# Recurrence and top-capacity experts on one core: 17 thresholds in the last search step, the recount dropped, five result buffers instead of three

## The chip, the core and the metric

The kernel runs on one core of a Trainium2 chip. Its engines run in parallel, each through its own queue in order: TensorE (PE for matmuls, PEld for weight loads), VectorE (DVE), ScalarE (ACT), GpSimd (POOL, which here issues the indirect transfers) and SyncE (SP). They wait for one another by semaphores. The metric is the device time of the whole kernel in microseconds, the median of several runs.

## The reference

A gated recurrence over 4 sequences of 5056 rows of 256, then a mixture of 8 experts in which each of the N = 20224 rows goes to one expert and each expert takes at most N/8 = 2528 rows. Pairs of row and expert are served in descending order of their logit, so an expert is full once its 2528 best rows are taken.

```python
sig = 1.0 / (1.0 + np.exp(-f_logit))
f = lower_bound[None, None, :] + (1.0 - lower_bound[None, None, :]) * sig
for t in range(S):
    h = f[:, t] * h + (1.0 - f[:, t]) * x[:, t];  y[:, t] = h
logits = y.reshape(B * S, D) @ w_gate
order = np.argsort(-logits.flatten())
for idx in order:
    tok, e = (int(idx) // E, int(idx) % E)
    if assigned[tok] >= 0 or counts[e] >= cap:
        continue
    assigned[tok] = e
    counts[e] += 1
for e in range(E):
    mask = assigned == e
    out[mask] = np.maximum(x[mask] @ w1[e], 0.0) @ w2[e]
```

## The kernel before

**First phase (to about 155 us).** Chunks of 512 rows are loaded, transposed, scanned, transposed back, written to a table in DRAM (`hbuf`) and their eight logits kept in SBUF (`X`, 128 partitions x 160 columns x 8 experts).

**Routing.** `route(k)` runs eight times. It finds the expert that fills up at the highest remaining threshold and the rows it takes. Each row has a best remaining expert (`argmax`, the one-hot `O`) and a 32-bit key of its logit. `search` finds the threshold by two levels of four steps: in each step the DVE compares all keys with 16 thresholds (`masks`, the tile `MK`, bf16), PE counts by 20 matmuls whose weights are 128 columns of MK (4 groups of columns x 16 thresholds x 2) and whose moving operand is 64 columns of `O`, and the DVE picks the step's next threshold. In the last step threshold 0 is taken from the float keys (`W <= wth`), a multiply with `selv` spreads the counts to `Z`, and one matmul with ones sums them over the partitions. `assign` marks the rows that are taken and counts them, ties by order; `compact` turns the marks into row numbers `ids`. `update` takes the full expert out (`pen` added to `X`) and lowers the room that is left of the others, `rE`: for that it counts again the rows above the threshold, by a mask `SB`, 20 matmuls with 8 weight columns of SB, a multiply with `bm8`, a reduction, and a matmul that sums over eight partitions (`CR` with `ones_r`).

**Experts.** Each expert has 2528 rows in chunks of up to four tiles of 128 rows, `CHUNKS`. A step is one chunk and one of 8 slices j of the hidden layer, 336 steps in all, and of PE's work in a step: `first` (layer one, 6 matmuls of up to 512 columns, into `pw`, made `hh` by ACT and `hl` by DVE), and for the step two back `second` (layer two, up to 12 matmuls of 256 columns, into `py`). Operands are split into high and low halves in fp32r. At j = 3 and j = 5 of a chunk, `trans` transposes the gathered rows (`xg`) of the next one on PE, right behind that step's `first`. In the third step of a chunk the results of the last chunk leave `py` by ACT into tiles `y`, two row tiles to a y.

**Order.** PE, DVE and ACT run in the order in which the code is written. The routing of later experts is cut into pieces (`yield`), and a planner (`Pace`, with guessed costs) puts a piece between the experts' matmuls when its inputs should be there. The first expert's search has nothing beside it, apart from filler matmuls (`busy`).

**POOL's transfers.** Gathers of rows, loads of weights and stores of results wait in one list, `issues`. Per step one is taken from its head, at the step's end (`issue(1, paced=True)`), and waits for the `hh` of that step (`gate[-1]`). Gathers of the chunk after next enter at j = 0, stores at the third step of a chunk, the three weight loads of an expert at the head. Transfers leave out of turn only in two places: `trans` first issues whatever of its chunk's gathers still stands in the list, and `second`, before it writes a new `y`, issues the stores of the y that is `YB` turns back. Those carry no wait for `hh`. In `yp` there are `YB` = 3 buffers for y, and `second` has

```python
issue(upto=lambda what: what[0] == "s" and what[1] <= turn - YB)
y = yp.tile([P, 2, D], F32, name="y")
```

Of the kernel before, what the change touches and what calls it, by code (L numbers as in the profile page):

```python
# [106 lines left out]
def kernel(ctx: ExitStack, tc: tile.TileContext, x: bass.AP, f_logit: bass.AP,  # L107
# [8 lines left out]
    CAP = N // E  # L116
# [111 lines left out]
    bm8 = consts.tile([P, 8, E], F32, name="bm8")  # L228
    lv.tensor_scalar(bm8, IO[:, :8].unsqueeze(2).to_broadcast([P, 8, E]), pv, None, op0=OP.is_equal)
# [12 lines left out]
    nc.gpsimd.memset(eighth, 0.125)  # L242
    j16 = consts.tile([P, 16, E], F32, name="j16")
# [26 lines left out]
    O = state.tile([P, NC, E], BF, name="O")  # L270
# [30 lines left out]
    W = state.tile([P, NC], F32, name="W")  # L301
    MK = state.tile([P, NG, 4, 16, 2], BF, name="MK")
# [3 lines left out]
    R16 = state.tile([P, NC], I16, name="R16")  # L306
    SB = state.tile([P, NC], BF, name="SB")
# [3 lines left out]
    Z = state.tile([P, 16, E], F32R, name="Z")  # L311
# [6 lines left out]
    wth = state.tile([P, 1], F32, name="wth")  # L318
# [43 lines left out]

    BZ = [11, 5, 12, 34, 8]
# [20 lines left out]
    def search(rt, first):  # L384
        steps = (4096.0, 256.0, 16.0, 1.0)
        for lev in range(2):
            val = (K16, R16)[lev]
            th = thr0
            for k in range(4):
                last = lev == 1 and k == 3  # L390
                done = first and lev == 0 and k == 0
                if not done:
                    for c in (0, 80):
                        if c and not first:
                            yield 'DVE',
# [24 lines left out]
                v.tensor_tensor(DM, ps[:, :64].rearrange("p (c e) -> p c e", e=E), bm, op=OP.mult)  # L420
                with nc.allow_low_precision(reason=EXACT):
                    v.tensor_reduce(CR, DM.rearrange("p c e -> p e c"), AX.X, OP.add)
                if last:
                    nc.gpsimd.memset(MKr[:, :, 0, :], 1.0)
                    v.tensor_tensor(Z, CR.bitcast(F32).unsqueeze(1).to_broadcast([P, 16, E]),
                                    selv.unsqueeze(2).to_broadcast([P, 16, E]), op=OP.mult)
# [11 lines left out]
                    return  # L438
# [15 lines left out]
                if k < 3:  # L454
                    th = TH[:, k % 2]
                    v.scalar_tensor_tensor(th, nn.unsqueeze(2).to_broadcast([P, 16, 2]), steps[k], PRE, op0=OP.mult,
                                           op1=OP.add)
                    if lev == 1 and k == 2:
                        v.tensor_scalar(wth, th[:, 0, 0:1], -1.0, -32768.0, op0=OP.mult, op1=OP.add)
# [9 lines left out]
    def assign(rt, first):  # L469
# [14 lines left out]
        ps = rt.tile([P, 512], F32, name="rt")  # L484
        nc.tensor.matmul(ps[:, 0:1], ones_b, cS, start=True, stop=False)
        nc.tensor.matmul(ps[:, 0:1], tri, cT, start=False, stop=True)
        yield 'DVE', ps
        v.tensor_scalar(lim, ps[:, 0:1], -1.0, float(CAP), op0=OP.mult, op1=OP.add)
# [11 lines left out]
    def compact(rt, ohp, ids, prog, first):  # L500
        v.tensor_tensor_scan(RS[:, :NT], onec[:, :NT], MS[:, :NT], 0.0, op0=OP.mult, op1=OP.add)
        yield 'PE', RS, cnt
        ps = rt[0].tile([P, 512], F32, name="rt")
# [16 lines left out]
        def place(k):  # L520
            nb = groups[k][1]
            ps = rt[k if first and k < 2 else 0].tile([P, 512], F32, name="rt")
# [63 lines left out]
    def update(rt, first):  # L586
        v.tensor_scalar(pen, kc, code, -BIG, op0=OP.is_equal, op1=OP.mult)
        v.tensor_scalar(SB, W, tlo, None, op0=OP.is_lt)
# [6 lines left out]
        yield 'PE', SB  # L595
        ps = rt.tile([P, 512], F32, name="rt")
# [6 lines left out]
        with nc.allow_low_precision(reason=EXACT):  # L603
            v.tensor_reduce(CR[:8], DM[:8].rearrange("p c e -> p e c"), AX.X, OP.add)
        v.tensor_scalar(Q8, kc, code, 1.0e9, op0=OP.is_equal, op1=OP.mult)
        v.tensor_add(rE, rE, Q8)
        yield 'PE', CR
        nc.tensor.matmul(ps[:, 64:64 + E], ones_r[:8, :], CR[:8], start=True, stop=True)
        yield 'DVE', ps
        v.tensor_sub(rE, rE, ps[:, 64:64 + E])  # L610
# [4 lines left out]
    def route(k, rt, wi, indexed, spawn):  # L615
        if k < E - 1:
# [4 lines left out]
            yield from search(rt, k == 0)  # L621
# [4 lines left out]
            yield from assign(rt, k == 0)  # L626
            spawn()
            yield 'DVE',
            yield from update(rt, k == 0)
# [125 lines left out]
def moe(ctx, tc, g):  # L755
# [12 lines left out]
    YB = 3  # L768
# [246 lines left out]
    def all_routes():  # L1015
        for k in range(E):
# [10 lines left out]
            def spawn():  # L1027
                assert k == 0 or comp[k - 1].done
                indexed()
                comp[k] = Bg(compact((rc, rt), ohp, IDS[k], prog[k], k == 0))  # L1030
# [123 lines left out]
```

## Time and profile before

| | us |
|---|---|
| median of three runs | 1202.95 (1202.89 to 1203.13) |
| the profiled execution | 1202.51 |
| its span, first to last instruction | 1200.7 |
| PE busy | 1172.0 (98% of the span) |
| DVE busy | 770.7 |
| ACT busy | 524.6 |
| POOL busy | 452.4 |

The time of the profiled execution is 1.8 us above its span: what lies before the first and behind the last instruction. In the page every instruction carries the line of the recording helper, L100, so instructions are told apart by their tiles. [...]

### The profile page before, as it was taken

Reading aid. Unit: us, or ns where it says so; the run is one execution under the profiler, and the core shown is the slowest. Engines: PE = TensorE matmul, PEld = TensorE weight load, DVE = VectorE, ACT = ScalarE, POOL = GpSimd, SP = SyncE. Lnnn points to the kernel's source line nnn. Section 1 sums busy time; section 2 is a strip of 40 time slices with the busy share of each in tenths; the row PEclk is TensorE's granted clock in tenths of the full one; section 3 lists DMA queues with packets and bytes.
Section 4 is the critical chain, followed back from the end, with each engine's and each line's share of the span. In section 5 each row is a group of like instructions: output and inputs, shape, how many; then the busy total and the mean of one; then the engine's idle time right before and its main releaser. Section 6 shows DMA issues by size and latency. Waiting matters only on the chain.

```text
span 1200.7 us, 23258 instructions
## 1 busy us (share of the span) xinstructions
PE 1172.0 (98%) x9152; PEld 1063.3 (89%) x9152; DVE 770.7 (64%) x1935; ACT 524.6 (44%) x1098; POOL 452.4 (38%) x458
## 2 busy tenths in 40 slices
PE   7999986999999999999999999999999999999997
PEld 7999965888988898888888888899889998999997
DVE  6999878878878977978788878423532243222222
ACT  7888813423533632632452345522642243223322
POOL 5777703332433324333333333333343334333322
PEclk9999998999999999999999999999999999999999
DMA  9999993112112212211211113111311131111111
GB/s 334 375 355 363 345 327 100 46 41 92 55 49 67 74 38 86 75 40 41 82 66 49 41 42 100 47 57 45 102 53 49 50 102 58 49 46 46 43 39 35
DMA packets 51869, 123.14 MB, mean 103 GB/s; under 512 B 7984, under 2 KB 28208, under 8 KB 50864
## 3 DMA queue, kind: packets, MB, share of 16 engines
q0 software_dynamic: 18960, 58.87, 15.7%
q1 hardware_dynamic: 32256, 62.78, 15.0%
q8 instruction: 72, 1.18, 0.4%
q14 instruction: 37, 0.30, 0.1%
q10 hardware_dynamic: 544, 0.01, 0.0%
HBM read 79.56 MB, written 42.07 MB: 101 GB/s over the span
## 4 chain that ended last, share of the span: by engine, by line
PE 61%; issue 19%; POOL 10%; DVE 4%; DMA 1%; POOLq 0%; ACT 0%; ACTq 0%; DVEq 0%; SPq 0%
PE py L100 25%; PE pw L100 24%; POOL out_dram L100 4%; POOL xg L100 4%; PE rt L100 4%; PE pr L100 4%; PE pb L100 2%; PE pf L100 2%; PE pt L100 1%; DVE MK L100 1%; POOL r L100 1%; DVE g L100 1%; DMA out_dram<-y,ids 0%; DMA fl<-in_f_logit_dram 0%; DMA xg<-hbuf,ids 0%
## 5 line engine op out<-in xcount | busy, mean ns | idle before, releaser
L100 PE MATMUL py<-w2s,hh 128*128 128x256 f32 (+1 forms) x2560 | 486.5, 287 | 0.6 <-ACT y L100 0.5
L100 ACT ACTIVATE hh<-pw 128x512 fp32r<-128x512 f32 (+3 forms) x336 | 192.5, 573 | 563.5 <-PE pw L100 541.2
L100 PEld LDWEIGHTS py<-w2s,hh 128*128 128x128 f32 (+1 forms) x2560 | 405.2, 187 | 19.2 <-ACT y L100 1.2
L100 DVE SCALAR_TENSOR_TENSOR hl<-pw,hh 128x512 fp32r<-128x512 f32 (+3 forms) x336 | 220.3, 656 | 313.7 <-ACT hh L100 312.6
L100 PE MATMUL py<-w2s,hl 128*128 128x256 f32 (+1 forms) x1280 | 361.3, 282 | 0.0
L100 POOL DMA_INDIRECT xg<-hbuf,ids x160 | 158.8, 992 | 313.9 <-ACT hh L100 292.6
L100 POOL DMA_INDIRECT out_dram<-y,ids x160 | 161.9, 1012 | 302.6 <-ACT hh L100 245.7
L100 PE MATMUL pw<-xh,w1h 128*128 128x512 f32 (+3 forms) x672 | 256.1, 383 | 2.4 <-DVE hl L100 1.7
L100 PE MATMUL pw<-xl,w1h 128*128 128x512 f32 (+3 forms) x672 | 257.7, 385 | 0.0
L100 PE MATMUL pw<-xh,w1l 128*128 128x512 f32 (+3 forms) x672 | 257.0, 384 | 0.0
L100 PEld LDWEIGHTS py<-w2s,hl 128*128 128x128 f32 (+1 forms) x1280 | 239.4, 187 | 0.0
L100 PEld LDWEIGHTS pw<-xh,w1l 128*128 128x128 f32 x672 | 125.9, 188 | 22.6
L100 PEld LDWEIGHTS pw<-xh,w1h 128*128 128x128 f32 x672 | 126.3, 189 | 14.4 <-DVE hl L100 1.9
L100 PEld LDWEIGHTS pw<-xl,w1h 128*128 128x128 f32 x672 | 126.0, 188 | 12.2 <-DVE r L100 0.2
L100 POOL TENSOR_TENSOR xl<-fl,xl 128x1024 f32<-128x1024 f32 (+1 forms) x39 | 92.3, 2366 | 42.8 <-ACT fl L100 35.1
L100 DVE TENSOR_TENSOR_SCAN g<-fg,g,pb 128x512 f32<-128x512 f32 (+4 forms) x78 | 92.8, 1227 | 9.9 <-ACT fg L100 8.9
L100 ACT ACTIVATE junk<-rt,r 128x158 bf16<-128x158 f32 x155 | 58.8, 392 | 53.9 <-DVE r L100 53.6
L100 PE MATMUL pr<-iw,g 128*128 128x136 f32 x632 | 79.8, 279 | 0.0
L100 PEld LDWEIGHTS pr<-iw,g 128*128 128x128 f32 x632 | 75.9, 190 | 0.1
L100 ACT ACTIVATE fg<-pf,one,nomlb 128x512 f32<-128x512 f32 (+1 forms) x80 | 57.4, 767 | 1.9
L100 ACT ACTIVATE y<-py 128x512 f32<-128x512 f32 (+2 forms) x88 | 48.1, 559 | 21.6 <-PE py L100 6.8
L100 DVE TENSOR_TENSOR xl<-pt,xh 128x512 fp32r<-128x512 f32 (+1 forms) x80 | 53.9, 674 | 0.6 <-ACT xh L100 0.3
(178 smaller groups left out, 1183.1 us busy)
## 6 DMA issues: line engine op xcount, KB each, us to landing
hbuf<-hr SPq DMA_DIRECT2D x39, 528.0 KB, 8.7
fl<-in_f_logit_dram SPq DMA_DIRECT2D x39, 512.0 KB, 5.9
xl<-in_x_dram SPq DMA_DIRECT2D x39, 512.0 KB, 6.1
xg<-hbuf,ids POOLq DMA_INDIRECT x160, 2.8
out_dram<-y,ids POOLq DMA_INDIRECT x160, 2.4
r<-in_moe_w_dram,wi POOLq DMA_INDIRECT x25, 4.5
hbuf<-hr SPq DMA_DIRECT2D x1, 264.0 KB, 9.1
fl<-in_f_logit_dram SPq DMA_DIRECT2D x1, 256.0 KB, 5.7
```

Of the source, the lines that this page charges most:

```text
L100: r = f(*args, **kw)
```

## The change

- **Last step of the search.** Columns are grouped by 7 instead of 8, with 17 thresholds: 23 groups of 7 x 17 = 119 slots, each padded to 128 columns of `MK`. Threshold 0 and the new threshold 16 come from the float keys by one comparison with a two-column `wth`, the other 15 from the 16-bit keys against `TL`, which repeats a threshold 7 times. PE counts by 23 matmuls of 128 weight columns and 56 moving columns. `s17` replaces `selv`; Z has 17 x 8 columns and its matmul 119 partitions.
- **No recount.** The count one threshold further is the number of rows strictly above: `update` picks it from the search's own PSUM tile by a multiply with a mask and a reduction, and subtracts it from `rE`. SB, its 20 matmuls and the sum over eight partitions are gone. The PSUM tile is therefore kept from the search through `assign` (which uses a column of it) to `update`, and the first `compact` takes its second tile from the pool `pws`.
- **Five buffers.** `YB` is 5.
- Constants: `bm8` goes; `d17`, `s17`, `t17`, `c7`, `bm7` and some fills of padding come.

```diff
-    MK = state.tile([P, NG, 4, 16, 2], BF, name="MK")
+    N7 = (NC + 6) // 7
+    MKb = state.tile([P, N7 * P], BF, name="MK")
+    MK = MKb[:, :NG * P].rearrange("p (g a t b) -> p g a t b", a=4, t=16, b=2)
+    MK8 = MKb.rearrange("p (g r) -> p g r", r=P)
+    MK7 = MK8[:, :, :119].rearrange("p g (t c) -> p g t c", c=7)
...
+    def fine(g0, g1):
+        n = g1 - g0
+        w, r = (x[:, 7 * g0:7 * g1].rearrange("p (g c) -> p g c", c=7) for x in (W7, R7))
+        v.tensor_tensor(MK7[:, g0:g1, 0::16, :], w.unsqueeze(2).to_broadcast([P, n, 2, 7]),
+                        wth.unsqueeze(1).unsqueeze(3).to_broadcast([P, n, 2, 7]), op=OP.is_le)
+        v.tensor_tensor(MK7[:, g0:g1, 1:16, :], r.unsqueeze(2).to_broadcast([P, n, 15, 7]),
+                        TL[:, 1:].unsqueeze(1).to_broadcast([P, n, 15, 7]), op=OP.is_ge)
...
-                        masks(val, th, c, c + 80, 1)
                         if last:
-                            v.tensor_scalar(MKr[:, c // 2:c // 2 + 40, 0, :],
-                                            W[:, c:c + 80].rearrange("p (g c) -> p g c", c=2), wth, None, op0=OP.is_le)
+                            fine(*((12, N7) if c else (0, 12)))
+                        else:
+                            masks(val, th, c, c + 80, 1)
...
-                for g in range(NG):
+                for g in range(N7 if last else 0):
+                    nc.tensor.matmul(ps[:, :56], MK8[:, g], O[:, 7 * g:7 * g + 7, :], start=(g == 0),
+                                     stop=(g == N7 - 1))
+                for g in range(0 if last else NG):
...
-                    nc.tensor.matmul(ps[:, 64:192], ones_r, Z.rearrange("p t e -> p (t e)"), start=True, stop=True)
+                    nc.tensor.matmul(ps[:, 64:200], ones_r[:119], Z[:119].rearrange("p t e -> p (t e)"), start=True,
+                                     stop=True)
...
-    def update(rt, first):
+    def update(ps, first):
         v.tensor_scalar(pen, kc, code, -BIG, op0=OP.is_equal, op1=OP.mult)
-        v.tensor_scalar(SB, W, tlo, None, op0=OP.is_lt)
+        v.scalar_tensor_tensor(GP, j16, n_, ps[:, 72:200].rearrange("p (t e) -> p t e", e=E), op0=OP.is_equal,
+                               op1=OP.mult)
+        v.tensor_reduce(Q8, GP.rearrange("p t e -> p e t"), AX.X, OP.add)
+        v.tensor_sub(rE, rE, Q8)
...
-        yield 'PE', SB
-        ps = rt.tile([P, 512], F32, name="rt")
-        for g in range(NG):
-            nc.tensor.matmul(ps[:8, :64], SB[:, 8 * g:8 * g + 8], O[:, 8 * g:8 * g + 8, :], start=(g == 0),
-                             stop=(g == NG - 1))
...
-        v.tensor_tensor(DM[:8], ps[:8, :64].rearrange("p (c e) -> p c e", e=E), bm8[:8], op=OP.mult)
-        with nc.allow_low_precision(reason=EXACT):
-            v.tensor_reduce(CR[:8], DM[:8].rearrange("p c e -> p e c"), AX.X, OP.add)
...
-        yield 'PE', CR
-        nc.tensor.matmul(ps[:, 64:64 + E], ones_r[:8, :], CR[:8], start=True, stop=True)
-        yield 'DVE', ps
-        v.tensor_sub(rE, rE, ps[:, 64:64 + E])
...
-    YB = 3
+    YB = 5
```

**DVE, last step of the first expert's search.** Before, the masks of 80 columns come as 16-bit part (`MK<-R`, 15 thresholds) and float part (`MK<-W`), twice:

```order
L100 SCALAR_TENSOR_TENSOR TH<-rt,PRE 128x32
L100 TENSOR_SCALAR wth<-TH 128x1
L100 TENSOR_TENSOR MK<-R_167,TH 128x40x30
L100 TENSOR_SCALAR MK<-W,wth 128x40x2
L100 TENSOR_TENSOR MK<-R_167,TH 128x40x30
L100 TENSOR_SCALAR MK<-W,wth 128x40x2
L100 TENSOR_SCALAR PRE<-TH 128x1
```

After:

```order
L100 SCALAR_TENSOR_TENSOR TL<-rt,PRE 128x112
L100 TENSOR_SCALAR wth<-TL 128x1 x2
L100 TENSOR_TENSOR MK<-W,wth 128x12x2x7
L100 TENSOR_TENSOR MK<-R_176,TL 128x12x105
L100 TENSOR_TENSOR MK<-W,wth 128x11x2x7
L100 TENSOR_TENSOR MK<-R_176,TL 128x11x105
L100 TENSOR_SCALAR PRE<-TL 128x1
```

The float part now stands ahead of the 16-bit part and has two thresholds; the halves are 12 and 11 groups of 7 columns.

**PE, the seventh expert's update,** behind the two matmuls that begin `compact` (`tri` and `nsub`). Before, up to the first of the twenty recounts (19 more pairs follow, then a step's `pw`):

```order
L100 LDWEIGHTS tri
L100 MATMUL rt<-cnt,tri 128x1
L100 LDWEIGHTS nsub
L100 MATMUL rt<-RS,nsub 128x160
L100 MATMUL py<-w2s,hh 128x256 x2
L100 MATMUL py<-w2s,hl 128x256
L100 LDWEIGHTS SB
L100 MATMUL rt<-O,SB 8x64
```

After:

```order
L100 LDWEIGHTS tri
L100 MATMUL rt<-cnt,tri 128x1
L100 LDWEIGHTS nsub
L100 MATMUL rt<-RS,nsub 128x160
L100 MATMUL pw<-xl,w1h 128x512
L100 MATMUL pw<-xh,w1l 128x512
L100 MATMUL py<-w2s,hh 128x256 x2
L100 MATMUL py<-w2s,hl 128x256
```

No SB stands in PE's order any more; the experts' matmuls follow one another, and the piece of routing has moved to another place in the step.

**POOL's transfers, from the fifth expert's fourth chunk to the sixth's first two** (buffer numbers kept; `96x264` is the last tile of an expert's rows, the gathers behind it are the sixth expert's). Before:

```order
L100 DMA xg_10319<-hbuf_65,ids_6715 128x264 x4
L100 DMA out_0_dram<-y_10407,ids_6715 20224x256
L100 DMA out_0_dram<-y_10420,ids_6715 20224x256
L100 DMA out_0_dram<-y_10694,ids_6715 20224x256 x2
L100 DMA out_0_dram<-y_10420,ids_6715 20224x256
L100 DMA xg_10628<-hbuf_65,ids_6715 128x264 x3
L100 DMA xg_10628<-hbuf_65,ids_6715 96x264
L100 DMA out_0_dram<-y_10684,ids_6715 20224x256 x2
L100 DMA xg_10844<-hbuf_65,ids_7908 128x264 x4
L100 DMA out_0_dram<-y_10900,ids_6715 20224x256 x2
L100 DMA out_0_dram<-y_10911,ids_6715 20224x256 x2
L100 DMA xg_11061<-hbuf_65,ids_7908 128x264 x4
```

After:

```order
L100 DMA xg_10145<-hbuf_65,ids_6653 128x264 x4
L100 DMA out_0_dram<-y_10216,ids_6653 20224x256 x2
L100 DMA out_0_dram<-y_10224,ids_6653 20224x256 x2
L100 DMA xg_10453<-hbuf_65,ids_6653 128x264 x3
L100 DMA xg_10453<-hbuf_65,ids_6653 96x264
L100 DMA out_0_dram<-y_10540,ids_6653 20224x256 x2
L100 DMA out_0_dram<-y_10548,ids_6653 20224x256 x2
L100 DMA xg_10714<-hbuf_65,ids_7801 128x264
L100 DMA xg_10929<-hbuf_65,ids_7801 128x264 x3
L100 DMA xg_10714<-hbuf_65,ids_7801 128x264 x3
```

Before, five stores stand between the first two groups of gathers and two between the next two, since some left out of turn; after, it is four each time, so four stores stand ahead of the sixth expert's first gathers (xg_10714) where two stood (xg_10844). Three gathers of the chunk behind (xg_10929), which `trans` issues out of turn, stand between them.

## Rows read from the trace of the kernel before

**Rows 1.** The table of busy time by stretch, three stretches of 50 us: the first expert's search (150 to 200), routing beside expert work (700 to 750), expert work alone (1100 to 1150). Columns: busy us of PE, PEld, DVE, ACT, POOL with instruction counts, the granted clock of TensorE as a share of full speed, the mean busy share of the DMA engines, GB/s.

```profile
150.00:200.00 50.00, 38.58 (x429) 30.94 (x428) 37.68 (x131) 8.00 (x16) 6.29 (x8) 0.93 0.73 225
700.00:750.00 50.00, 50.00 (x414) 44.18 (x413) 40.47 (x131) 24.11 (x59) 16.71 (x17) 1.00 0.24 76
1100.00:1150.00 50.00, 50.00 (x329) 45.34 (x328) 14.71 (x22) 14.51 (x25) 16.86 (x18) 1.00 0.15 45
```

**Rows 2.** The timeline of PE alone around the recount of one `update`, 735 to 737 us. Columns: start us, us (to the modelled end of the last of the merged matmuls), engine, line, operation, out<-in, tile, count. What an instruction keeps from the next is the distance from its start to the next start.

```profile
735.30 0.28 PE L100 MATMUL py<-w2s,hl 128*128 128x256 f32 x1
735.51 0.75 PE L100 MATMUL rt<-O,SB 128*8 128x64 bf16 x20
736.19 0.50 PE L100 MATMUL pw<-xh,w1h 128*128 128x512 f32 x1
736.52 0.39 PE L100 MATMUL pw<-xl,w1h 128*128 128x512 f32 x1
```

**Rows 3.** The same view around the sum over the recount's eight partitions, 294 to 297 us; the first two rows show an ordinary pair of starts.

```profile
294.43 0.28 PE L100 MATMUL py<-w2s,hl 128*128 128x256 f32 x1
294.55 0.39 PE L100 MATMUL pw<-xh,w1h 128*128 128x512 f32 x1
...
295.24 0.39 PE L100 MATMUL pw<-xh,w1h 128*128 128x512 f32 x1
295.56 0.27 PE L100 MATMUL rt<-CR,onesr 8*128 8x8 f32 x1
295.76 0.50 PE L100 MATMUL pw<-xl,w1h 128*128 128x512 f32 x1
296.09 0.39 PE L100 MATMUL pw<-xh,w1l 128*128 128x512 f32 x1
```

**Rows 4.** The same view around the twenty counting matmuls of the search's last step, 723 to 725 us.

```profile
723.42 0.40 PE L100 MATMUL pw<-xh,w1h 128*128 128x512 f32 x1
723.66 0.76 PE L100 MATMUL rt<-O,MK 128*128 128x64 bf16 x20
724.25 0.48 PE L100 MATMUL pw<-xl,w1h 128*128 128x512 f32 x1
724.57 0.40 PE L100 MATMUL pw<-xh,w1l 128*128 128x512 f32 x1
```

**Rows 5.** The same view around the matmul that sums Z over the 128 partitions, 725 to 726.5 us.

```profile
725.39 0.28 PE L100 MATMUL py<-w2s,hl 128*128 128x256 f32 x1
725.51 0.22 PE L100 MATMUL rt<-Z,onesr 128*128 128x128 f32 x1
725.58 0.45 PE L100 MATMUL py<-w2s,hh 128*128 128x256 f32 x2
725.86 0.28 PE L100 MATMUL py<-w2s,hl 128*128 128x256 f32 x1
```

**Rows 6.** The timeline of all engines in the last step of the first expert's search, 183 to 186 us, of which the DVE rows of the masks and the PE row of the second half's counting matmuls stand here.

```profile
183.38 0.19 DVE L100 SCALAR_TENSOR_TENSOR TH<-rt,PRE 128x32 int16<-128x32 f32 x1 [0.26 <-PE rt L100]
183.60 0.15 DVE L100 TENSOR_SCALAR wth<-TH 128x1 f32<-128x1 int16 x1
183.67 0.77 DVE L100 TENSOR_TENSOR MK<-R,TH 128x1200 bf16<-128x1200 int16 x1
184.36 0.26 DVE L100 TENSOR_SCALAR MK<-W,wth 128x80 bf16<-128x80 f32 x1
184.53 0.78 DVE L100 TENSOR_TENSOR MK<-R,TH 128x1200 bf16<-128x1200 int16 x1
...
185.54 0.47 PE L100 MATMUL rt<-O,MK 128*128 128x64 bf16 x10 [0.40 <-DVE PRE L100]
```

**Rows 7.** Groups of DVE instructions by form: names, shapes, count | busy us, mean ns of one | idle us before.

```profile
L100 DVE TENSOR_TENSOR X<-X,pen 128x640 f32<-128x640 f32 x14 | 11.3, 815 | 0.0
...
L100 DVE SCALAR_TENSOR_TENSOR GP<-GP,sc,kc 128x128 f32<-128x128 f32 x7 | 2.4, 345 | 0.0
...
L100 DVE TENSOR_TENSOR asg<-asg,TI 128x160 f32<-128x160 f32 x6 | 2.0, 336 | 0.2
```

**Rows 8.** ACT's wait for a store in the list of who waited for whom (us in total, times, longest).

```profile
ACT y L100 <- DMA out_dram<-y,ids: 6.2, 3, 2.3
```

**Rows 9.** The timeline of PE alone at one of those three waits, 626 to 628 us.

```profile
626.67 0.27 PE L100 MATMUL py<-w2s,hl 128*128 128x256 f32 x1
627.22 0.50 PE L100 MATMUL py<-w2s,hh 128*128 128x256 f32 x2 [0.28 <-ACT y L100]
```

**Rows 10.** The timeline of all engines, 800 to 805 us, of which these rows stand here: the first of the two layer-two matmuls after a step's layer one, that step's hh on ACT, the gather that POOL then issues, the last layer-one matmul of the next step, the four transposes behind it, and what PE does next.

```profile
801.13 0.40 PE L100 MATMUL py<-w2s,hh 128*128 128x256 f32 x2
...
801.33 0.60 ACT L100 ACTIVATE hh<-pw 128x512 fp32r<-128x512 f32 x1 [2.24 <-PE pw L100]
...
802.20 0.98 POOL L100 DMA_INDIRECT xg<-hbuf,ids  x1 [1.84 <-ACT hh L100]
...
803.72 0.39 PE L100 MATMUL pw<-xh,w1l 128*128 128x512 f32 x1
...
803.95 0.43 PE L100 MATMUL pt<-identr,xg 128*128 128x128 f32 x4
...
804.22 0.49 PE L100 MATMUL py<-w2s,hh 128*128 128x256 f32 x2
```

**Rows 11.** The tile xg (a chunk's gathered rows): time from the issue of its 160 gathers to their landing.

```profile
DMA to landing us min/median/max: 2.7/2.8/3.8
```

More of the change, by code (lines that the diff above doesn't have):

```diff
@@ L242 @@
     nc.gpsimd.memset(eighth, 0.125)
+    d17 = consts.tile([P, 17], F32, name="d17")
+    nc.gpsimd.iota(d17, pattern=[[-7, 17]], base=0, channel_multiplier=1, allow_small_or_imprecise_dtypes=True)
+    s17 = consts.tile([P, 17], F32, name="s17")
+    t17 = consts.tile([P, 17], F32, name="t17")
+    nc.gpsimd.tensor_scalar(t17, d17, -6.0, None, op0=OP.add)
+    nc.gpsimd.tensor_mul(s17, t17, d17)
+    lv.tensor_scalar(s17, s17, 0.0, None, op0=OP.is_le)
+    lv.tensor_tensor(t17, s17, d17, op=OP.mult)
+    c7 = consts.tile([P, 1], F32, name="c7")
+    lv.tensor_reduce(c7, t17, AX.X, OP.add)
+    bm7 = consts.tile([P, 7, E], F32, name="bm7")
+    lv.tensor_scalar(bm7, IO[:, :7].unsqueeze(2).to_broadcast([P, 7, E]), c7, None, op0=OP.is_equal)
     j16 = consts.tile([P, 16, E], F32, name="j16")
@@ L269 @@
     TMP = state.tile([P, NC, E], F32, name="TMP")
-    O = state.tile([P, NC, E], BF, name="O")
+    O = state.tile([P, NC + 1, E], BF, name="O")
     asg = state.tile([P, NC], F32, name="asg")
@@ L300 @@
     KL = state.tile([P, NC], F32, name="KL")
-    W = state.tile([P, NC], F32, name="W")
-    MK = state.tile([P, NG, 4, 16, 2], BF, name="MK")
+    W7 = state.tile([P, NC + 1], F32, name="W")
+    W = W7[:, :NC]
+    nc.gpsimd.memset(W7[:, NC:], 0.0)
+    N7 = (NC + 6) // 7
[3 more added lines that the diff above has]
+    MK7 = MK8[:, :, :119].rearrange("p g (t c) -> p g t c", c=7)
+    nc.gpsimd.memset(MKb[:, NG * P:], 0.0)
     MKr = MK.rearrange("p g a t b -> p (g a) t b")
@@ L305 @@
     K16 = state.tile([P, NC], I16, name="K16")
-    R16 = state.tile([P, NC], I16, name="R16")
-    SB = state.tile([P, NC], BF, name="SB")
+    R7 = state.tile([P, NC + 1], I16, name="R16")
+    R16 = R7[:, :NC]
+    nc.gpsimd.memset(R7[:, NC:], 0.0)
     TH = state.tile([P, 2, 16, 2], I16, name="TH")
@@ L310 @@
     DM = state.tile([P, 8, E], F32, name="DM")
-    Z = state.tile([P, 16, E], F32R, name="Z")
+    Z = state.tile([P, 17, E], F32R, name="Z")
     GP = state.tile([P, 16, E], F32, name="GP")
@@ L317 @@
     sc = state.tile([P, 4], F32, name="sc")
-    wth = state.tile([P, 1], F32, name="wth")
+    wth = state.tile([P, 2], F32, name="wth")
+    TL = state.tile([P, 16, 7], I16, name="TL")
     MS = state.tile([P, NC], F32, name="MS")
@@ L437, in search @@
                     v.tensor_reduce(code, GP, AX.XY, OP.max)
-                    return
+                    return ps
+                v.tensor_tensor(DM, ps[:, :64].rearrange("p (c e) -> p c e", e=E), bm, op=OP.mult)
+                with nc.allow_low_precision(reason=EXACT):
+                    v.tensor_reduce(CR, DM.rearrange("p c e -> p e c"), AX.X, OP.add)
                 yield 'PE', CR
@@ L454, in search @@
                 if k < 3:
[L455 to L459, printed above, removed]
+                    fin = lev == 1 and k == 2
+                    th, cols = (TL, 7) if fin else (TH[:, k % 2], 2)
+                    v.scalar_tensor_tensor(th, nn.unsqueeze(2).to_broadcast([P, 16, cols]), steps[k],
+                                           PRE[:, :, 0:1].to_broadcast([P, 16, cols]), op0=OP.mult, op1=OP.add)
+                    if fin:
+                        for j in range(2):
+                            v.tensor_scalar(wth[:, j:j + 1], th[:, 0, 0:1], -1.0, -32768.0 - 16 * j, op0=OP.mult,
+                                            op1=OP.add)
                 else:
@@ L467, in weights_index, with assign @@
         v.scalar_tensor_tensor(wi, wk, code, wb, op0=OP.mult, op1=OP.add)
-    def assign(rt, first):
+    def assign(ps, first):
         if first:
@@ L483, in assign @@
             busy(BZ[2])
-        ps = rt.tile([P, 512], F32, name="rt")
-        nc.tensor.matmul(ps[:, 0:1], ones_b, cS, start=True, stop=False)
-        nc.tensor.matmul(ps[:, 0:1], tri, cT, start=False, stop=True)
+        nc.tensor.matmul(ps[:, 208:209], ones_b, cS, start=True, stop=False)
+        nc.tensor.matmul(ps[:, 208:209], tri, cT, start=False, stop=True)
         yield 'DVE', ps
-        v.tensor_scalar(lim, ps[:, 0:1], -1.0, float(CAP), op0=OP.mult, op1=OP.add)
+        v.tensor_scalar(lim, ps[:, 208:209], -1.0, float(CAP), op0=OP.mult, op1=OP.add)
         v.scalar_tensor_tensor(TI, TR, lim, TI, op0=OP.is_le, op1=OP.mult)
@@ L502, in compact @@
         yield 'PE', RS, cnt
-        ps = rt[0].tile([P, 512], F32, name="rt")
+        ps = rt[0][0].tile([P, 512], F32, name=rt[0][1])
         nc.tensor.matmul(ps[:, 160:161], tri, cM, start=True, stop=True)
@@ L521, in place @@
             nb = groups[k][1]
-            ps = rt[k if first and k < 2 else 0].tile([P, 512], F32, name="rt")
+            pool, name = rt[k if first and k < 2 else 0]
+            ps = pool.tile([P, 512], F32, name=name)
             for b in range(nb):
@@ L620, in route @@
                 yield from keys(0, NC)
-            yield from search(rt, k == 0)
+            ps = yield from search(rt, k == 0)
             weights_index(wi)
@@ L625, in route @@
                 yield 'DVE',
-            yield from assign(rt, k == 0)
+            yield from assign(ps, k == 0)
             spawn()
             yield 'DVE',
-            yield from update(rt, k == 0)
+            yield from update(ps, k == 0)
             updated[k] = True
@@ L1029, in spawn @@
                 indexed()
-                comp[k] = Bg(compact((rc, rt), ohp, IDS[k], prog[k], k == 0))
+                comp[k] = Bg(compact(((rc, "rt"), (pws, "pw")), ohp, IDS[k], prog[k], k == 0))
             yield from route(k, rt, WI[k], indexed, spawn)
```

20 lines of the change are left out of this document (9 added, 11 removed).

## The prediction

> **What bounds the kernel now.** I read the table of busy time by stretch first. Beside routing and in the experts alone PE is busy 50.00 of 50 us at full clock, DVE 40.47 and 14.71 [rows 1]: from about 205 us on, PE sets the pace. So whatever takes PE's time there counts one to one, and another engine counts only where PE waits for it. The first expert's search (150 to 200 us) is different: PE is busy for 38.58 of 50 us, fillers among it, and the chain runs from DVE to PE and back, so each instruction of that chain counts. Then I read PE's timeline around the instructions that the change removes, by distances between starts; then the two kinds of transfer that PE can come to wait for, stores (through ACT's copies to y) and gathers (through the transposes).
>
> **Recount removed, on PE.** From the py matmul at 735.30 to the second pw at 736.52 it is 1.22 us with the 20 SB pairs between [rows 2]. Without them a py start is 0.12 from the next (294.43 to 294.55 [rows 3]) and a 512-column pw 0.23 (803.72 to 803.95 [rows 10]), so 0.35. One recount costs 0.87, seven 6.1 us. The first expert's stands at 213 us, in PE's full stage as well. The sum over eight partitions, CR with onesr: 295.24 to 296.09 is 0.85, two pw would take 0.46, so 0.39 each, seven 2.7 us [rows 3]. Together **8.8 us less**.
>
> **17 thresholds, on PE.** Twenty counting pairs take 0.59 from the first start to the next pw (723.66 to 724.25), 0.03 a pair [rows 4]; three more cost 0.09, for six experts **0.5 more** (the first expert's are in the chain below). 56 moving columns instead of 64 I take as no gain: the pair with 8 weight columns (SB) is not shorter than the one with 128. The Z matmul costs now 0.19 less 0.12, and 0.04 in the pair behind (0.28 instead of two times 0.12), 0.11 in all [rows 5]. With 119 partitions the nearest row is that of 128; the far bound is that of 8 partitions, 0.39, and 2.0 more in seven. I take 0.
>
> **The first expert's last step, on DVE.** Before, from TH (183.38) to PE's start on the second half (185.54) it is 2.16 us [rows 6]. After: TL has 112 columns instead of 32, between the 0.19 of TH [rows 6] and the 0.345 of 128 columns [rows 7], so 0.13 more than TH's 0.22 to the next start; two wth at 0.07 (183.60 to 183.67); the float part 168 and 154 elements of two sources, nearest 160 in 0.336 [rows 7], started 0.09 before its end as now, 0.25 and 0.24; the 16-bit part 1260 elements, 0.72 by the 0.69 that 1200 take from start to start, and 1155 to its end, 0.75, and 0.05 to PE. Sum 2.49, and one pair of the second half more: **0.4 more**. That is if seven columns to a run go as fast as two. If not, the bound is the fp32 rate, 640 elements in 0.815 and 160 in 0.336 [rows 7], so 1.0 ns each, 1.43 and 1.33 us, and the step is 1.2 longer still. [...]
>
> In the later experts the DVE stands beside a full PE: about 0.3 us more per expert for the masks, and in update the SB mask, two instructions on eight partitions and one subtraction go, a multiply, a reduction and a subtraction come, some 0.8 us either way. DVE has 9 of 50 us free [rows 1]; I count 0. The kept PSUM tile costs nothing, since the next search takes it only after update has read it, and the second tile of the first compact stands free in pws before layer one begins.
>
> **Five buffers, the store side.** With three, ACT waited three times for a store, 6.2 us in total, 2.3 the longest [rows 8]. PE felt part of it: 626.67 to 627.22 is 0.55 instead of 0.12, and the pair behind is 0.50 long instead of 0.40 [rows 9], so 0.5 for the longest. For three I take **1.3 less** (bounds 0.5 and 1.6).
>
> **Five buffers, the gather side.** This is the large term. Per step one transfer leaves the list, and a four-tile chunk brings eight in eight steps, so the list never shrinks by itself, and each expert's three weight loads lengthen it. Before, the stores that YB = 3 forced out of turn shortened it: I followed the list through the code step by step, and the last gather of a chunk left two to ten steps ahead of its transposes. With YB = 5 no store is forced any more. The list is longer by then, four stores stand ahead of the sixth expert's first gathers instead of two, and in this steady state a chunk's four gathers leave at j = 7, 0, 1 and 2, while PE transposes at j = 3. That holds for 19 chunks (three of the fourth expert, four each of the fifth to eighth), and for one of the first expert. The second chunks of the fourth to seventh expert escape, since `trans` finds three of their gathers (one in the fourth) in the list and those carry no wait for hh, so they run early.
>
> What one step ahead means stands in one place of the trace [rows 10]. Layer one of a step ends at 801.13, its hh at 801.93, and the gather that waits for it starts on POOL at 802.20. (Before, that gather was for a much later chunk.) It lands 2.8 us later by the median [rows 11], at 805.00. PE is at the next step's transposes at 803.95, at the fourth, which needs this tile, at 804.15. So PE would wait 0.85 us, and nothing stands in for it, as PE runs in order and everything behind is experts' work. In 13 of the 19 chunks nothing else stands between on PE: 11.3 us (0.85, or 0.92 behind a chunk with a 96-row tile). In five a routing piece of 0.1 to 0.3 does: about 0.7 each, 3.5. In one a counting burst covers the wait. The first expert's takes 0.9. PE's restart costs up to 0.1 more, as behind the wait in [rows 9]; I take 0.05, 1.0 in all. Together **16.7 more**. With the shortest landing of 2.7 it is 14, with the full restart and some landings nearer to 3.8, 19.
>
> **Sum.** 8.8 and 1.3 less, 0.5, 0.4 and 16.7 more: 7.5 us more than the profiled execution's 1202.5, 1210.0; the median lies 0.4 above that execution, so **1210.4 us**.
>
> **Rivals.**
> - *The gathers land in time.* Then the recount's gain stays: 9.2 less, 1193.7 us, faster. It would need a gather that takes under 2 us to land or leaves ahead of its hh. The bound from which the sign turns is 0.48 us of waiting per chunk, a landing of 2.4 us, below the shortest of 160 [rows 11]. For it speaks only that before no PE wait for a gather of a later expert is seen, so none has been measured. 0.12.
> - *Half of the waits.* If routing pieces fall into the waits, or the transposes stand later in the step than I read, the two sides cancel: about 1202, within 0.2%. 0.05.
> - *Masks at half speed.* Runs of seven at the fp32 rate: 1.2 in the first expert, and 1.3 per later expert that DVE's free time covers: 1211.6. [...] Chance 0.10.
> - *The sum over 119 partitions costs like that over eight,* so the new step gives back part of what it saves: 2.0 more, 1212.4. 0.07.
> - [...] A step of 0.4 is little; I give it no chance of its own, and up to 2 us of the range.
>
> **How the numbers follow.** The forecast has 0.66, with its own range of 1206 to 1214 (waits of 14 to 19, restart, clock). The two dearer forms lie within it. Leaving out the first two rivals, 0.17, the range is **1205.5 to 1214.5**. 0.2% is 2.4 us, about what a measurement of this kernel can tell from no change: faster 0.12, same 0.05, slower 0.83.
>
> **What would show it.** PE's list of waits should have a new entry, transposes waiting for the DMA of xg, some 20 times and 14 to 17 us in total, and PE's busy time in the stretches after 800 us should fall to 48 of 50. No SB and no 8-partition matmul should stand in the trace, and ACT's wait for stores should be gone. The MK masks should take about 0.81 and 0.76 (1.4 and 1.3 if at half speed). I am wrong if PE stays at 50 of 50 after 800 us: then the gathers were early, and the time is near 1194.

## The result and the profile after

The changed kernel takes 1210.3 us (1209.33 to 1210.49, six runs), the kernel before beside it 1202.45 (1201.88 to 1203.13): ratio 1.0062, 95% interval 1.0051 to 1.0072. That is 7.9 us more, slower, where 1210.4 was forecast. The profiled execution took 1210.49, its span is 1208.7, 8.0 above that of the one before.

The same three stretches as in [rows 1], of the changed kernel:

```profile
150.00:200.00 50.00, 39.63 (x433) 31.61 (x432) 37.71 (x132) 8.12 (x17) 6.02 (x9) 0.90 0.74 229
700.00:750.00 50.00, 49.66 (x418) 44.41 (x417) 41.09 (x129) 23.86 (x56) 15.40 (x16) 1.00 0.23 76
1100.00:1150.00 50.00, 48.67 (x319) 43.91 (x318) 14.36 (x21) 14.70 (x25) 16.33 (x17) 1.00 0.14 43
```

In the experts alone, where nothing was edited but the number of buffers, PE now stands still for 1.33 of 50 us, at full clock. The list of who waited for whom (us in total, times, longest) has the reason. Before, it had one wait of PE's weight loads for gathered rows:

```profile
PEld pt L100 <- DMA xg<-hbuf,ids: 1.1, 1, 1.1
```

After:

```profile
PEld pt L100 <- DMA xg<-hbuf,ids: 16.0, 20, 1.3
...
PE pt L100 <- DMA xg<-hbuf,ids: 13.2, 20, 1.2
```

These are the same 20 waits twice, at the weight load and at the matmul of a transpose; added up they would be counted double. One of the 20 stands at 202 us, ahead of layer one, where the kernel before has its one (200.4 us). So 19 are new: one in the first expert (226 us) and 18 from 622 us on. ACT's wait for stores [rows 8] is not in the list any more. One of the 18 in the timeline of all engines, 822.5 to 828 us:

```profile
822.84 0.40 PE L100 MATMUL py<-w2s,hh 128*128 128x256 f32 x2
823.04 0.57 ACT L100 ACTIVATE hh<-pw 128x480 fp32r<-128x480 f32 x1 [2.18 <-PE pw L100]
...
823.88 0.94 POOL L100 DMA_INDIRECT xg<-hbuf,ids  x1 [0.97 <-ACT hh L100]
...
825.37 0.38 PE L100 MATMUL pw<-xh,w1l 128*128 128x480 f32 x1
825.59 0.36 PE L100 MATMUL pt<-identr,xg 128*128 128x128 f32 x3
...
826.70 0.28 PE L100 MATMUL pt<-identr,xg 128*128 128x128 f32 x1 [0.75 <-DMA xg<-hbuf,ids]
826.82 0.47 PE L100 MATMUL py<-w2s,hh 128*128 128x256 f32 x2
```

It reads as [rows 10], but the gather that waits for this hh is now the one that the next step's transposes need. Layer one of a step ends, ACT makes hh (823.04 to 823.61), POOL issues the chunk's last gather at 823.88. PE's wait for it ends 2.8 us later, which is also the median landing in this trace. PE is through the next step's layer one and three of four transposes by 825.8 and starts the fourth at 826.70. From the start of the first three to that of the fourth it is 1.11 us, where three transposes take 0.2.

PE around the seventh expert's update, in place of [rows 2]:

```profile
742.46 0.40 PE L100 MATMUL pw<-xh,w1h 128*128 128x512 f32 x1
742.70 0.18 PE L100 MATMUL rt<-cnt,tri 128*128 128x1 bf16 x1
742.74 0.23 PE L100 MATMUL rt<-RS,nsub 128*128 128x160 bf16 x1
742.76 0.48 PE L100 MATMUL pw<-xl,w1h 128*128 128x512 f32 x1
743.08 0.40 PE L100 MATMUL pw<-xh,w1l 128*128 128x512 f32 x1
```

Neither SB nor a sum over eight partitions follows. PE at the 23 counting matmuls, in place of [rows 4], and at the sum over 119 partitions, in place of [rows 5]:

```profile
729.60 0.77 PE L100 MATMUL rt<-O,MK 128*128 128x56 bf16 x23
730.21 0.48 PE L100 MATMUL pw<-xh,w1l 128*128 128x512 f32 x1
730.53 0.39 PE L100 MATMUL pw<-xh,w1h 128*128 128x512 f32 x1
...
731.93 0.23 PE L100 MATMUL rt<-Z,onesr 119*128 119x136 f32 x1
732.00 0.45 PE L100 MATMUL py<-w2s,hh 128*128 128x256 f32 x2
732.28 0.28 PE L100 MATMUL py<-w2s,hl 128*128 128x256 f32 x1
```

Twenty-three pairs take 0.61 to the next pw, where twenty took 0.59. The sum takes 0.07 to the next start and 0.28 for the pair behind, as with 128 partitions. DVE in the last step of the first expert's search, in place of [rows 6]:

```profile
184.33 0.27 DVE L100 SCALAR_TENSOR_TENSOR TL<-rt,PRE 128x112 int16<-128x112 f32 x1 [0.25 <-PE rt L100]
184.64 0.22 DVE L100 TENSOR_SCALAR wth<-TL 128x1 f32<-128x1 int16 x2
184.89 0.34 DVE L100 TENSOR_TENSOR MK<-W,wth 128x168 bf16<-128x168 f32 x1
185.14 0.90 DVE L100 TENSOR_TENSOR MK<-R,TL 128x1260 bf16<-128x1260 int16 x1
185.96 0.31 DVE L100 TENSOR_TENSOR MK<-W,wth 128x154 bf16<-128x154 f32 x1
186.18 0.84 DVE L100 TENSOR_TENSOR MK<-R,TL 128x1155 bf16<-128x1155 int16 x1
```

The 16-bit part takes 0.90 and 0.84 us: more than the 0.81 and 0.76 that were forecast, far from the 1.43 and 1.33 of half speed. From TL to PE's start on the second half (187.08) it is 2.75 us, before 2.16.

**Where the 8.0 us come from.** For each matmul of PE, from the first of layer one to the last of the kernel, I took the distance to the next start, less what the same matmul has undisturbed (0.12 for py, 0.23 for a pw of 512 columns, 0.07 for a transpose), and put the excess down to what stands there. The excess of the pairs right ahead of and right behind a routing matmul counts as that matmul's:

| | before | after | change | forecast |
|---|---|---|---|---|
| SB pairs | 6.10 | 0 | -6.1 | -6.1 |
| CR with onesr | 2.76 | 0 | -2.8 | -2.7 |
| counting pairs (MK) | 31.92 | 32.43 | +0.5 | +0.5 |
| Z with onesr | 0.67 | 0.58 | -0.1 | 0 |
| transposes (waits for xg) | 1.99 | 17.75 | +15.8 | +16.7 |
| layer two (waits for y) | 6.31 | 5.25 | -1.1 | -1.3 |
| all excess, the rest included | 73.10 | 79.55 | +6.45 | |
| start of layer one | 201.49 | 203.01 | +1.5 | +0.4 |

6.45 and 1.52 are the 7.97 of the spans.

### The profile page after: what moved, and what is told of

Same layout as the page of the kernel before. It is cut to its first block, busy times and chain, and to the rows that moved or that the text cites. A ratio compares the mean times of both kernels' runs of the same rounds, so it can differ in the third digit from the quotient of the medians.

```text
span 1208.7 us, 23006 instructions
## 1 busy us (share of the span) xinstructions
PE 1168.2 (97%) x9026; PEld 1060.6 (88%) x9026; DVE 778.7 (64%) x1938; ACT 527.9 (44%) x1098; POOL 449.9 (37%) x464
## 4 chain that ended last, share of the span: by engine, by line
PE 51%; issue 27%; POOL 14%; DVE 4%; DMA 3%; POOLq 0%; ACT 0%; SPq 0%; ACTq 0%; DVEq 0%
PE py L100 19%; PE pw L100 17%; POOL xg L100 7%; POOL out_dram L100 6%; PE pr L100 5%; PE rt L100 3%; PE pb L100 3%; PE pf L100 2%; DMA xg<-hbuf,ids 2%; DVE g L100 1%; DVE MK L100 1%; PE pt L100 1%; DMA hbuf<-hr 1%; POOL r L100 1%; DMA xl<-in_x_dram 1%
## 5 line engine op out<-in xcount | busy, mean ns | idle before, releaser
L100 PEld LDWEIGHTS pt<-identr,xg 128*128 128x128 f32 (+1 forms) x320 | 36.3, 140 | 25.0 <-DMA xg<-hbuf,ids 16.0
```

Source lines behind the costliest of these rows:

```text
L100: r = f(*args, **kw)
```

## The experiments

Runs of one batch stand beside runs of the kernel before on the same chip; it took 1205.4 us there for the first four, 1202.4 for the next four, so differences are compared, not times.

| run | us | before | difference | ratio, 95% interval |
|---|---|---|---|---|
| e1, changed, three buffers | 1200.64 | 1205.37 | -4.7 | 0.9961 (0.9947 to 0.9974) |
| e2, before, five buffers | 1220.64 | 1205.37 | +15.3 | 1.0133 (1.0118 to 1.0149) |
| e3, changed, forced at three | 1199.49 | 1205.37 | -5.9 | 0.9950 (0.9936 to 0.9963) |
| e4, before, five, forced at three | 1203.07 | 1205.37 | -2.3 | 0.9983 (0.9974 to 0.9992) |
| e5, changed again | 1210.03 | 1202.42 | +7.6 | 1.0063 (1.0049 to 1.0077) |
| e6, changed, four buffers | 1208.64 | 1202.42 | +6.2 | 1.0054 (1.0041 to 1.0068) |
| e7, changed, two transfers a step | 1195.80 | 1202.42 | -6.6 | 0.9943 (0.9929 to 0.9957) |
| e8, forced at three, two in the first expert | 1194.19 | 1202.42 | -8.2 | 0.9929 (0.9916 to 0.9943) |

**e1, three buffers in the changed kernel.**

```diff
-    YB = 5
+    YB = 3
```

> The changed kernel with three buffers for y in place of five; all else stays. My theory (five buffers end the forced stores, the list of transfers stays longer, and the last gather of a chunk leaves one step ahead of its transposes): read from the instructions, the gap is one step in 1 chunk here (the first expert's), in 20 with five buffers. So 19 waits of 14.2 us go and the store waits of 1.3 us come back: 1210.3 - 14.2 + 1.3 = 1197.4 us, PE at 50 of 50 us in the stretches after 800 us. Rival (the shorter routing makes the steps shorter and the gathers late, whatever the buffers): the waits stay, 1210 to 1212 us.

4.7 us below the kernel before, 5.1 expected. Of the 19 new waits one is left, the first expert's, 1.33 us, beside the one ahead of layer one; ACT waits for stores again (10.1 us, 5 times).

```profile
PEld pt L100 <- DMA xg<-hbuf,ids: 2.6, 2, 1.3
```

The rival falls: with the new routing and three buffers no later expert waits.

**e2, five buffers in the kernel before.**

```diff
-    YB = 3
+    YB = 5
```

> The kernel before with five buffers for y; the old routing with its recount stays. My theory: the gap from last gather to transposes is one step in 19 chunks, all of the fourth to eighth expert; they wait 14.2 us, the store waits of 1.3 us go: 1202.5 + 14.2 - 1.3 = 1215.4 us. Rival (the waits come with the new routing): 1201 us. Second rival (half of the waits were due to where the new routing's pieces stand): 1208 us.

15.3 us above, 12.9 expected. The old routing with five buffers has the waits too (same view and columns as above):

```profile
PEld pt L100 <- DMA xg<-hbuf,ids: 17.5, 18, 2.1
...
PE pt L100 <- DMA xg<-hbuf,ids: 14.9, 18, 1.9
```

One of these 18 is again the one ahead of layer one, 17 are in the experts. So the waits come with the buffers, also without the new routing, and both rivals fall. Three of the waits are longer than any in the changed kernel, 1.7 to 2.1 us; one of them in the timeline of all engines, 826.5 to 835 us:

```profile
830.69 0.57 ACT L100 ACTIVATE hh<-pw 128x480 fp32r<-128x480 f32 x1 [3.32 <-PE py L100]
831.53 0.94 POOL L100 DMA_INDIRECT xg<-hbuf,ids  x1 [2.09 <-ACT hh L100]
...
834.39 0.28 PE L100 MATMUL pt<-identr,xg 128*128 128x128 f32 x1 [1.92 <-DMA xg<-hbuf,ids]
```

Here hh itself ends at 831.26, 0.84 before the transposes begin (832.10), against 1.98 in the changed kernel's wait above (823.61 to 825.59); it comes late on ACT, and the gather that is tied to it with it. The row has ACT waiting for layer-two matmuls (py) there, which stands in two of the three waits and in no other run; why is not shown. These three took 3.4 us more than 0.8 each; the sum was 2.4 short.

**e3, five buffers, but stores still forced out at three turns.**

```diff
-                issue(upto=lambda what: what[0] == "s" and what[1] <= turn - YB)
+                issue(upto=lambda what: what[0] == "s" and what[1] <= turn - 3)
```

> The changed kernel with five buffers, but the stores of the y three turns back are still forced out before a new y is written, as with three buffers. My theory (it is the forced store, not the number of buffers, that keeps the list short): the gap is one step in 1 chunk only, so the 14.2 us go and the store waits stay away: 1196.1 us, 1.3 less than with three buffers. Rival (buffers and lists have nothing to do with it; ACT and PE run further ahead of the transfers with five buffers): 1210 us.

5.9 us below the kernel before and 1.2 below e1. PE is at 50.00 of 50 us in both of these stretches:

```profile
800.00:850.00 50.00, 50.00 (x338) 45.57 (x338) 17.56 (x40) 18.55 (x44) 16.68 (x18) 1.00 0.23 71
1100.00:1150.00 50.00, 50.00 (x328) 45.32 (x327) 14.58 (x22) 15.13 (x26) 16.46 (x17) 1.00 0.15 45
```

Five buffers as such cost nothing; what costs is that they took the forced store away. In this run's profile TensorE's clock fell to about half of full speed (0.51) from 208.1 to 211.5 us, in the first expert's layer one:

```profile
208.00:211.50 3.50, 3.50 (x21) 3.40 (x19) 1.88 (x5) 0.77 (x3) 0.00 (x0) 0.51 0.17 43
```

From 207.3 to 212.8 us the excess is 1.9 us, where the profiles of the result and of the other runs up to e8 have 0.6 to 0.8 at this place. PE had stood still for 1.8 us before 206.8, but in the profiles of the kernel before and of the result it does so for 1.7 and 1.8 us at this place, and there the clock is 1.00 from 208 to 211.5. So the profiled execution has lost 1.3 us here that no term covers; how many of the other four did is not on record.

**e4, the same in the kernel before,** both edits of e2 and e3.

> The kernel before with five buffers and the store of the y three turns back still forced out: the store side by itself. My theory: ACT's wait for stores (6.2 us, three times) goes, of which PE felt 1.3 us: 1201.2 us. Rival (what PE lost there is found again at the next wait): 1202.5 us. Together with the run of the changed kernel that forces at three it gives the new routing by itself: 1201.2 - 1196.1 = 5.1 us, of which the terms were 8.8 less, 0.1 and 0.6 more in the first expert's search and the counting, 1.4 for the first expert's one wait, and 0.9 by which the first phase ended later in the profiled run.

2.3 us below, 1.3 expected; ACT's waits for stores are gone. In its profile the excess at layer two falls by 1.5 us (6.31 to 4.77, the first number from the profile of the kernel before, which is of the batch of the result); the rest I can't put down to anything. The new routing by itself, e3 against e4, is 3.6 us, 5.1 expected (and 5.8 by the terms that the expectation lists). Two losses of e3's profile lie in that difference: the 1.3 us at half clock (above), and one place in the sixth expert's last step, which the timeline of all engines shows, 647.5 to 653.5 us:

```profile
648.17 0.77 PE L100 MATMUL rt<-O,MK 128*128 128x56 bf16 x23
...
650.63 0.22 DVE L100 TENSOR_TENSOR DM<-rt,bm 119x56 f32<-119x56 f32 x1 [2.30 <-PE pw L100]
...
651.52 0.33 PE L100 MATMUL rt<-Z,onesr 119*128 119x136 f32 x1 [1.11 <-DVE Z L100]
```

The counting matmuls are over before 649, DVE takes them up at 650.63, and PE waits 1.3 us for Z. A burst is a row of counting matmuls. Behind the last-step bursts of the other experts DVE takes the counts up 0.2 to 1.1 us after the start of the last matmul, and in e7 and e8 behind this one too. e1 has the same delay in the same place. See the last section.

**e5, the changed kernel again.**

> The changed kernel once more, beside the next three on one chip, since the kernel before took 1205.4 us on the chip of the first four runs and 1202.5 on that of the result. Expected: 7.4 us above the kernel before (ratio 1.0062), whatever the chip, if the waits for gathers are a matter of the order of transfers. Rival (the waits depend on the chip's speed of landing): 5 or 10 us.

7.6 us above, 7.4 expected; the result repeats itself, with the same 20 waits. The record gives e1 to e8 one chip number, 3, so the 3 us between the two batches' runs of the kernel before are not shown to come from the chip, and the rival about the chip's speed was not put to the test.

**e6, four buffers.**

```diff
-    YB = 5
+    YB = 4
```

> The changed kernel with four buffers for y. Read from the instructions, the gap from last gather to transposes is one step in 16 chunks in place of 20: the four of the fourth and fifth expert that go waited 0.71, 0.14, 0.73 and 0.51 us in the changed kernel. My theory (each such chunk costs its own wait): 2.1 us less than the changed kernel of this batch, up to 0.5 given back by a store wait. Rival (a buffer more or less has an effect of its own, half way from three to five): 6 us less.

1.4 us less than e5, with runs from 1207.7 to 1209.9; in the profiles the excess at the transposes falls from 17.99 to 15.82, by 2.2, where 2.1 was expected; the rival's 6 us less falls. The four waits of the fourth and fifth expert are gone, the others are there (0.7 to 0.93 us each). So the price is counted by chunks whose last gather leaves one step ahead, not by buffers.

**e7, two transfers a step while the list is long.**

```diff
-        issue(1 if i < len(todo) else 99, paced=i < len(todo))
+        issue(99 if i >= len(todo) else 2 if len(issues) > 8 else 1, paced=i < len(todo))
```

> The changed kernel with five buffers and no forced stores, but a step takes two transfers from the list instead of one while it holds more than eight. Read from the instructions the gap is one step in 1 chunk, five and more in all others. My theory (the length of the list is the cause, and any way to shorten it does): the waits of 14.2 us go, 13 to 14 us less than the changed kernel, the same as with forced stores, 6 us below the kernel before. Rival (two transfers behind one hh stand in each other's way on POOL, which takes about 1 us for each, or in the DMA engines): the gathers land later and half of the waits or more stay.

14.2 us less than e5. No store is forced and five buffers stay, and of the 19 new waits only the first expert's (1.34 us) is left. Two transfers behind one hh don't hurt here.

```profile
PEld pt L100 <- DMA xg<-hbuf,ids: 2.1, 2, 1.3
```

**e8, stores forced at three turns, and two transfers a step in the first expert's first two chunks.** To e3:

```diff
-        issue(1 if i < len(todo) else 99, paced=i < len(todo))
+        issue(99 if i >= len(todo) else 2 if k == 0 and c < 2 else 1, paced=i < len(todo))
```

> The changed kernel with five buffers, the stores forced out at three turns, and in the first two chunks of the first expert two transfers a step in place of one, since there the gap of one step was left (1.3 us of PE's wait at 225 us). Read from the instructions no chunk has a gap under three steps. My theory: 1.3 us less than with forced stores alone, 7.2 us below the kernel before (ratio 0.994). Rival (the first expert's transfers then collide with those of the weights, and the wait moves on): 5.9 us below, as with forced stores alone.

8.2 us below the kernel before, 15.8 below the changed one, the fastest of all. The excess at the transposes is 1.91 (3.27 in e7, 1.99 in the kernel before): no wait of PE for xg is left but the one ahead of layer one.

**e9, two prices by themselves.**

```diff
+                v.tensor_tensor(p7, r7, t7, op=OP.is_ge)
...
+                v.tensor_tensor(p8[:, :, :, :7], r8[:, :, :7].unsqueeze(2).to_broadcast([P, 12, 15, 7]),
+                                t8[:, :, :7].unsqueeze(1).to_broadcast([P, 12, 15, 7]), op=OP.is_ge)
...
+            for q in (8, 32, 64, 119, 128):
+                yield 'PE', CR
+                nc.tensor.matmul(ps[:, 216:216 + E], ones_r[:q], CR[:q], start=True, stop=True)
```

> Two prices by themselves, in the kernel of the run before (five buffers, forced stores), with instructions added whose results nothing reads: in the first expert's update four forms of the 16-bit comparison, twice each; in the updates of the next six experts one more sum with ones over 8, 32, 64, 119 and 128 partitions with 8 columns, and one over 8 partitions with 136. The time is therefore longer and of no interest. Comparison: the packed form of the change (12 groups x 15 x 7 = 1260 elements) took 0.90 us. If the odd run costs (the last element of a run goes alone), 7 of 8 aligned columns take 0.90 too, 8 of 8 (1200 elements) 0.78, 6 of 8 (1080) about 0.70. If the odd start costs (every other run begins off a 4-byte border), 7 of 8 take 0.81. Sum: if it is the small number of partitions that cost 0.39 in the old update, the distance to the next start grows by 0.39 with 8, with 8 and 136 columns even more, and by 0.1 with 119 and 128; 32 and 64 show from where. If the old 0.39 came from something else in that place, all five cost 0.1.

DVE's four forms, in the groups by form (busy us, mean ns of one): 7 of 8 columns, 7 packed, 8 of 8, 6 of 8.

```profile
L100 DVE TENSOR_TENSOR SCR<-R,T 128x1260 bf16<-128x1260 int16 x2 | 1.9, 974 | 0.0
L100 DVE TENSOR_TENSOR SCR<-R,TL 128x1260 bf16<-128x1260 int16 x2 | 1.8, 906 | 0.0
L100 DVE TENSOR_TENSOR SCR<-R,T 128x1200 bf16<-128x1200 int16 x2 | 1.6, 782 | 0.0
L100 DVE TENSOR_TENSOR SCR<-R,T 128x1080 bf16<-128x1080 int16 x2 | 1.4, 718 | 0.0
```

The two even forms give 0.064 us for 120 elements, so 1260 of them would take 0.81, and 1440 (180 runs of eight) 0.91. The packed runs of seven take 0.906: as long as runs of eight, by the odd run. Aligned starts don't help; with them (7 of 8 columns) it is 0.974, which neither expectation has, and why it is more than 0.906 is not shown. PE's timeline at the second expert's sums, 306 to 310 us:

```profile
306.33 0.40 PE L100 MATMUL pw<-xh,w1h 128*128 128x512 f32 x1
306.65 0.27 PE L100 MATMUL rt<-CR,onesr 8*128 8x8 f32 x1
306.85 0.50 PE L100 MATMUL pw<-xl,w1h 128*128 128x512 f32 x1
307.19 0.40 PE L100 MATMUL pw<-xh,w1l 128*128 128x512 f32 x1
...
309.17 0.28 PE L100 MATMUL py<-w2s,hl 128*128 128x256 f32 x1
309.28 0.17 PE L100 MATMUL rt<-CR,onesr 119*128 119x8 f32 x1
309.31 0.49 PE L100 MATMUL py<-w2s,hh 128*128 128x256 f32 x2
309.63 0.29 PE L100 MATMUL py<-w2s,hl 128*128 128x256 f32 x1
```

With 8 partitions it is 0.86 from the pw ahead to the one after next, 0.40 more than two pw; with 119, 0.46 from the py ahead over the pair behind, 0.10 more than three py. Worked out so over six experts, disturbed places left out, 8, 32 and 64 partitions cost 0.39 to 0.41 each, 119 and 128 between 0.08 and 0.12, 8 partitions with 136 columns 0.45 to 0.47.

## Why the prediction was right, point by point

- **Recount and sum over eight partitions:** 8.9 us, 8.8 forecast. Distances between starts, with the pair behind, gave the price to a tenth; e9 shows that the 0.39 was indeed that of few partitions.
- **Three more pairs:** 0.5 as forecast, but by luck. 23 pairs take 0.61, 0.02 more than 20 with 0.59, not 0.09: a pair with 56 moving columns took 26 ns, one with 64 took 30. The step that failed is "56 moving columns instead of 64 I take as no gain"; the pairs it was read from, SB, differ in weight columns and have the same 64 moving ones. The rest of the 0.5 is in the experts' pairs next to the bursts: of the 48 bursts beside the experts 46 now stand right ahead of experts' work, 45 before.
- **119 partitions:** cost what 128 do. The rival of 2.0 falls, and e9 shows why one row of the trace (8 partitions) was no neighbour of 119: the price steps between 64 (0.39 to 0.41) and 119 (0.08 to 0.12). What makes the step is not shown.
- **First expert's last step:** 0.6, 0.4 forecast. Against the forecast the odd run cost 0.1 more in each half, the two wth together 0.1 more. The rival of half speed falls: its 1.43 was an estimate from the float rows of [rows 7], and 0.90 was measured. Aligned starts gained nothing in e9 (0.974 against 0.906), and at the rate of the two even forms 1260 elements would take 0.81, where e9 has 0.91.
- **Start of layer one, the term that was missing:** 1.5 us later, of which the step explains 0.6. In the profiled run the first phase ended 0.96 later: the first mask over its last columns stands at 158.34 on DVE, against 157.38. Behind that, nothing but the last step differs: the first and the last thresholds that DVE sets there lie 22.52 us apart in both traces, and from the sum of Z to layer one it is 14.54 in both. In e5, the same kernel, the mask stands at 157.38, and TensorE's clock then fell for a few microseconds, to 0.57 of full speed in one window of 4 us. Windows of 176 to 180 us, of the changed kernel's first profile and of e5's:

```profile
176.00:180.00 4.00, 3.36 (x42) 2.33 (x39) 2.77 (x10) 0.00 (x0) 0.00 (x0) 1.00 1.03 316
```

```profile
176.00:180.00 4.00, 4.00 (x37) 3.15 (x36) 2.26 (x6) 0.00 (x0) 0.00 (x0) 0.57 0.92 281
```

At 0.57 PE is busy all the time (the clock is 0.55 and 0.59 in the two halves), and that step of the search took 1.0 longer. e8 has such a fall at 176 us too (0.50 and 0.68 in the same halves). Over the profiles, layer one began at 202.3 to 203.2 with the new routing (seven), at 201.2 to 201.7 with the old (three). So the step is shown; what lies beyond it is a later end of the first phase in the profiled run, and the fall of the clock in e5 and e8. Whether the change brings these about or they are spread stays open. The 2 us of the range that the prediction gave the clock are a term that no run shows: TensorE's clock is 0.50 from 192 to 198 us in the profile of the kernel before and from 190 to 199 in that of the changed one, and there it is 1.00 again from 199.2, ahead of layer one at 203.0.
- **Store side:** 1.1, 1.3 forecast; e4 shows it alone, 2.3 by the times and 1.5 in the profile.
- **Gather side:** 15.8, 16.7 forecast, the decisive term. e1, e2, e3 and e7 tell it apart four ways: fewer buffers, the old routing, forced stores, a shorter list. The nineteen chunks took 14.2 us (0.93 to 0.51 each, 0.14 the one that a counting burst covers) where 14.8 and 0.95 of restart were forecast: no restart is seen as a cost of its own. The first expert's took 1.36, not 0.9. PE is busy 48.7 to 49.3 of 50 us in the stretches from 800 to 1150 us, where the sign named was 48.
- **The rivals with the gathers in time, or half of the waits,** fall with the list of waits.

The terms that were off, 0.9 too much on the gather side and 1.1 too little in the first expert's stage, nearly cancel. That the forecast, 1210.4, lies 0.1 from the measured time is luck; that the gathers decide, and by about 16 us, is not.

## What to carry to other kernels

A buffer that has to be freed also sets the order: here the wait for a free y was what pushed stores out of turn and kept a one-per-step list short, and two more buffers let it grow until the last gathers of 20 chunks left one step ahead of their use. Before a pool grows, follow what its reuse triggers, count for each consumer how many steps ahead its transfer leaves, and compare that with one landing; where both are wanted, keep the trigger and grow the pool (e8). And when several edits go in together, take them apart: the recount's 8.9 us were there all the time, hidden under 15.8 us from one number.

## What the hardware showed that was not expected

- **A matmul with weights on 8, 32 or 64 partitions** cost 0.39 to 0.41 us in a stream of 128-partition ones, on 119 or 128 partitions 0.08 to 0.12 (e9, at 8, 32, 64, 119 and 128 partitions). With 8 partitions, 136 moving columns cost 0.06 more than 8.
- **Odd inner runs of 16-bit elements** took the time of the next even ones in the one length tried: 180 packed runs of seven 0.906 us, 180 runs of eight 0.91 as worked out from two even forms.
- **DVE sometimes took up a finished count late.** In the first four runs and in e9, 0.3 us and more after the last counting matmul's start in 50 of 151 places where DVE was free, against 0.2 elsewhere; once 1.9 us (e3, above, and e1 in the same place). In all 50 POOL was issuing an indirect transfer, was about to within 0.2 us, or had ended one less than 0.8 us before; but so it was in 42 of the other 101. In the profiles of the result and of e5 to e8 no such delay is seen, with nearly the same instructions. The batches with the delay are those in which the kernel before takes about 1205 us (1205.37, and 1204.99 beside e9), those without it have it at 1202.4. What differs between them was not tried, and how much of the 3 us the delay makes up is not shown, since no profile of the kernel before is from a batch with it.
